# Output stores of a state-space convolution and gated-MLP kernel: one transfer over 128 partitions instead of four over 32

## The chip, the cores and the metric

One core of one Trainium2 chip. The metric is the device time of one execution in microseconds; of the kernel before there are three runs, and their median is used.

## The reference

The input `A_q` (here `x`) has 2,048 tokens of 640 numbers, in bfloat16. The result is the sum of three terms:

```python
x = A_q
xn = _layernorm(x, axis=-1)
return x + _A_ref(xn, A_k, A_v, A_shift_k, A_ssm_k, A_ssm_D) + _B_ref(xn, B_w_gate, B_w_up, B_w_down)
```

`_A_ref` shifts `k` over four tokens with weights, multiplies it by `v`, convolves each of the 640 channels over all 2,048 tokens by a Fourier transform, adds a skip term, and multiplies by `xn`. `_B_ref` is a gated MLP: `g = xn @ w_gate`, `u = xn @ w_up`, `h = sigmoid(g) * u`, `h @ w_down`, with 1,728 hidden columns. The output has the shape and type of `x`: 2,048 x 640 in bfloat16, 2.62 MB.

## The kernel before, in words

**Layout.** The tile `acc` (line 259) lives in SBUF during the whole kernel. It has 128 partitions, 16 token tiles `m` and 640 columns. It is loaded with `x`, the two branches are added into it, and at the end it is stored to the output. The tokens are not laid out in plain order: token = 64 n + 16 q + m, where n runs to 32, q to 4, m to 16, and the partition is p = 32 q + n. The convolution needs this order. One partition therefore holds 16 tokens that follow each other in DRAM, so that several token tiles of one partition form one run of bytes (1,280 bytes a tile). The views `xq4` and `oq4` of input and output are written so:

```python
xq4 = A_q.flatten_outer_dims().rearrange("(n q m) d -> q n m d", q=4, m=NQ)
oq4 = out.flatten_outer_dims().rearrange("(n q m) d -> q n m d", q=4, m=NQ)
```

In DRAM the row of partition (q, n) begins at 10240 q + 40960 n elements. Within one q all 32 rows have one distance; over all 128 partitions, two distances are needed.

**Stages.** TensorE runs two streams that are interleaved: the convolution as Fourier matrices (lines 508, 528, 580 and 612), and the MLP, four token groups of 512 tokens, each with 14 pieces of hidden columns (gate and up, line 770) and then the down projection (line 786). ScalarE and VectorE empty PSUM. What reaches `acc` last are VectorE's additions: line 621 adds the convolution's product for four token tiles and half the columns, and line 798 adds 320 columns of one token tile's down projection.

**Order.** Every operation is recorded with what it reads and writes, then emitted in the order of a list written out by hand (`ORDER`, lines 80 to 124), in which numbers 960 to 983 are the stores. So the order on each engine's queue is fixed. A DMA is issued by SyncE (queue SP), or by ScalarE (queue ACT) where `q="ACT"` is given. Each queue issues in order: an instruction that waits holds up all behind it. The framework hands out eight completion semaphores to the DMAs in turn, and a DMA waits until the transfer that had its semaphore before has completed.

**The stores.** `store` (line 626) is called six times (lines 891 to 896): token tiles 0 to 7, 8 to 11, 12 and 13, 14, and tile 15 in two halves of 320 columns. Each call issues four DMAs, one for each q, of 32 partitions; for the halves of tile 15, q = 1 and 3 are issued by ScalarE. In `ORDER` two of the four stores of tiles 8 to 11 stand late, among those of tile 14. On SyncE the built program has, in this order: one store of tiles 0 to 7, one of 8 to 11, three of 0 to 7, one of 8 to 11, four of 12 and 13, one of 14, one of 8 to 11, three of 14, one of 8 to 11, and four of tile 15. The first store of tile 14 has a completion semaphore that a ScalarE store of tile 15 uses before it.

**Two small loads with the same kind of view.** `load_D` (line 394) and `load_shift` (line 380) read views with the group g (4) outermost, into four partitions 32 apart:

```python
srow = A_shift_k.rearrange("(h g d) m -> g h (d m)", h=2, g=G)
drow = A_ssm_D.rearrange("(h g d) -> g h d", h=2, g=G)
```

**Other transfers that the text names.** `xnd<-xq` (line 692) writes the normalized tokens to a buffer in DRAM, from 128 partitions. `P<-S` (line 548) copies half a tile, 64 partitions, to the other half within SBUF. `w<-in_B_w_up_dram` and `w<-in_B_w_gate_dram` (line 378) load 512 columns of weights into 128 partitions, five runs each.

Of the kernel before, what the change touches and what calls it, by code (L numbers as in the profile page):

```python
# [15 lines left out]
ACT = mybir.ActivationFunctionType  # L16
# [26 lines left out]
def _dft_tables():  # L43
# [74 lines left out]
    395, 396, 545, 895, 921, 896, 907, 546, 900, 923, 908, 922, 910, 559, 924, 912, 547, 548, 560, 561, 563, 564, 562,  # L118
    565, 913, 566, 569, 567, 915, 909, 568, 570, 579, 911, 925, 580, 914, 933, 582, 917, 572, 916, 934, 581, 583, 935,
    919, 584, 573, 918, 575, 574, 576, 586, 920, 944, 577, 960, 938, 587, 939, 589, 945, 402, 593, 941, 588, 590, 591,  # L120
    966, 962, 594, 947, 936, 963, 596, 942, 937, 943, 595, 961, 597, 965, 598, 940, 946, 403, 970, 969, 948, 950, 949,
    952, 968, 951, 953, 954, 971, 956, 973, 967, 975, 974, 972, 955, 964, 957, 958, 979, 978, 976, 977, 959, 982, 983,
    981, 980
]
ON_DVE = [
    101, 103, 133, 134, 135, 136, 656, 658, 884, 875, 525, 518, 915, 570, 581, 575
# [93 lines left out]
def kernel(  # L220
# [17 lines left out]
    oq4 = out.flatten_outer_dims().rearrange("(n q m) d -> q n m d", q=4, m=NQ)  # L238
# [20 lines left out]
    acc = cst.tile([P, NQ, DM], BF16, name="acc")  # L259
# [61 lines left out]
    def dma(fn, nd, run, q="SP", **kw):  # L321
        few = 1.4 if nd <= 64 and run > 1000 else 1.0
        plan.op({q: (0.48 + nd / 8000.0, lambda: fn(nc.sync if q == "SP" else nc.scalar))},
                size=1.05 * few * nd * (10.6 + run / 23.8) / 16e3 + 0.03, **kw)
# [301 lines left out]
    def store(m0, m1, pri, d0=0, d1=DM):  # L626
        key = [("acc", m, x) for m in range(m0, m1) for x in range(4)] if d1 - d0 == DM else (
            [("fin", m, d0 // 320) for m in range(m0, m1)] + [("cv", m // 4) for m in range(m0, m1)])
        for q in range(4):
            dma(lambda e, q=q: e.dma_start(oq4[q][:, m0:m1, d0:d1], acc[32 * q:32 * q + 32, m0:m1, d0:d1]), 32,  # L630
                2 * (d1 - d0) * (m1 - m0), q="ACT" if m0 == 15 and q % 2 else "SP", r=key, w=[("out", m0, d0, q)], pri=pri)

    MEAN, VAR, RST, TMP, EPS = range(5)

# [247 lines left out]
    for tr in range(4):  # L882
# [5 lines left out]
        if tr < 3:  # L888
            rec_tp(tr + 1, gt())
        rec_down(tr, tr == 3)  # L890
    store(0, 8, 240.0)
    store(8, 12, 242.0)
    store(12, 14, 244.0)
    store(14, 15, 246.0)
    store(15, 16, 247.0, d1=320)
# [32 lines left out]
```

## Time and profile before

| | us |
|---|---|
| median of 3 runs | 259.51 (258.78 to 261.09) |
| profiled execution, its own time | 262.01 |
| its span, first to last instruction | 259.9 |
| TensorE busy | 244.0 (94%) |
| VectorE busy | 201.2 (77%) |
| ScalarE busy | 175.5 (68%) |
| last matmul ends, last addition ends | 252.2, 252.7 |
| mean granted TensorE clock | 0.978 |

The span is what the views of the profile count in: their times start with the first instruction. The profiled execution's own time is 2.1 us longer than its span. In its page one of 40 slices, before 182 us, has a granted TensorE clock of 0.5; the slices around it have 0.9 or more. Busy shares are over the whole span. A row of DMA issues gives the number of transfers of one size, the KB of each and the median time from issue to landing (the last completion); it gives none where no landing could be read. The share of 16 DMA engines is the time that packets took, divided by 16 times the stretch.

### The profile page before, as it was taken

The page shows a single profiled execution, that of the slowest core. Times are in us where ns is not written, and L with a number is a line of the kernel's source. Part 1 is how long each engine was busy: PE and PEld are TensorE (multiplying, and loading weights), DVE is VectorE, ACT ScalarE, POOL GpSimd, SP SyncE. Part 2 cuts the span into 40 slices and gives each one's busy share as a digit, 9 for nine tenths or more (in the row PEclk, how much of TensorE's full clock was granted, in tenths as well). Part 3 has the DMA queues.
Part 4 walks back from the last instruction along what each step waited for, and adds up shares of the span by engine and source line. Part 5 has one row for each costly group of instructions (what it writes and reads, how often), then busy time and mean ns, then how long its engine had stood idle before and what let it go on. Part 6 is the DMA issues. An engine that isn't in the chain of part 4 may idle for free.

```text
span 259.9 us, 9463 instructions
## 1 busy us (share of the span) xinstructions
PE 244.0 (94%) x4231; PEld 146.1 (56%) x4231; DVE 201.2 (77%) x337; ACT 175.5 (68%) x259; POOL 0.7 (0%) x6
## 2 busy tenths in 40 slices
PE   8999979999999999999999997899999999998980
PEld 2854436764445467666554554577676554556750
DVE  4623524768999899999999999579999998895630
ACT  3623779767888899788998885663899785441100
POOL 1000000000000000000000000000000000000000
PEclk9999999999999999999999999599999999999996
DMA  6999999999995528999999739934126476002823
GB/s 175 310 277 207 205 314 130 152 139 188 229 248 128 143 75 235 150 140 128 157 182 283 192 66 318 188 101 117 23 62 177 99 236 184 1 5 55 188 73 95
DMA packets 91024, 41.44 MB, mean 159 GB/s; under 512 B 66656, under 2 KB 88104, under 8 KB 90664
## 3 DMA queue, kind: packets, MB, share of 16 engines
q1 hardware_dynamic: 90600, 40.44, 73.6%
q8 instruction: 33, 0.54, 0.9%
q10 hardware_dynamic: 384, 0.41, 0.5%
q14 instruction: 7, 0.06, 0.1%
HBM read 30.61 MB, written 5.24 MB: 138 GB/s over the span
## 4 chain that ended last, share of the span: by engine, by line
PE 64%; DMA 18%; DVE 5%; SPq 4%; issue 3%; ACT 3%; DVEq 0%; ACTq 0%
PE g L786 25%; PE g L770 25%; DMA acc<-in_A_q_dram 9%; PE c L528 6%; DMA w<-in_B_w_up_dram 5%; DMA vt<-in_A_v_dram 3%; PE c L612 3%; PE c L580 3%; PE c L508 2%; DMA P<-S 2%; ACT S L314 1%; SPq L378 1%; SPq L352 1%; DVE hT L737 1%; SPq L827 1%
## 5 line engine op out<-in xcount | busy, mean ns | idle before, releaser
L770 PE MATMUL g<-xnT,w 128*128 128x512 bf16 x380 | 90.9, 379 | 2.6 <-ACT sig L735 1.3
L786 PE MATMUL g<-wd,hT 128*128 128x320 bf16 x448 | 68.5, 306 | 2.0 <-issue 2.0
L770 PEld LDWEIGHTS <-w 128*128 128x128 bf16 x380 | 34.7, 98 | 41.1 <-issue 2.6
L786 PEld LDWEIGHTS <-hT 128*128 128x128 bf16 x448 | 42.6, 99 | 19.4 <-issue 2.3
L314 ACT CAST S<-c 128x1024 bf16<-128x1024 f32 x40 | 39.4, 1026 | 8.1 <-PE c L528 8.0
L737 DVE TENSOR_TENSOR hT<-sig,g 128x512 bf16<-128x512 bf16 x32 | 21.9, 686 | 18.6 <-PE g L770 18.3
L770 PE MATMUL g<-xnT,V 128*128 128x512 bf16 x140 | 32.8, 379 | 0.0
L735 ACT ACTIVATE sig<-g 128x512 bf16<-128x512 f32 x32 | 19.2, 601 | 15.1 <-PE g L770 13.5
L798 DVE TENSOR_TENSOR acc<-g,acc 128x320 bf16<-128x320 f32 x32 | 15.5, 488 | 17.4 <-PE g L786 17.2
L528 PEld LDWEIGHTS <-Mt 64*128 64x128 f16 x1280 | 20.2, 96 | 8.7 <-issue 8.1
L528 PE MATMUL c<-T,Mt 64*128 64x64 bf16 x1280 | 22.8, 191 | 2.2 <-issue 2.2
L317 ACT ACTIVATE T<-c 128x1024 bf16<-128x1024 f32 x20 | 19.9, 1029 | 5.5 <-PE c L508 5.4
L770 PEld LDWEIGHTS <-V 128*128 128x128 bf16 x140 | 13.3, 98 | 15.7 <-DMA V<-in_B_w_up_dram 0.5
L488 DVE TENSOR_TENSOR kvt<-ta,vt 128x1024 bf16<-128x1024 bf16 x10 | 21.4, 2143 | 0.1
L314 ACT CAST V<-c 128x1024 bf16<-128x1024 f32 x18 | 18.2, 1026 | 3.2 <-PE c L580 3.1
L314 ACT CAST T<-c 128x1024 bf16<-128x1024 f32 x19 | 18.8, 1024 | 1.6 <-PE c L508 1.4
L729 ACT ACTIVATE sig<-g 128x512 bf16<-128x512 f32 x18 | 10.8, 602 | 5.0 <-PE g L770 3.3
L561 DVE TENSOR_TENSOR S<-S 128x1024 bf16<-128x1024 bf16 x20 | 13.8, 688 | 0.3
L475 DVE TENSOR_TENSOR ta<-ta,tb 128x1024 bf16<-128x1024 bf16 x20 | 13.8, 688 | 0.3
L470 DVE TENSOR_TENSOR tb<-kt,sT 128x1024 bf16<-128x1024 bf16 x20 | 13.8, 690 | 0.1
L567 DVE TENSOR_TENSOR S<-P 64x1024 bf16<-64x1024 bf16 x18 | 12.4, 689 | 0.6
L565 DVE TENSOR_TENSOR S<-S 64x1024 bf16<-64x1024 bf16 x18 | 12.4, 687 | 0.6
(82 smaller groups left out, 240.9 us busy)
## 6 DMA issues: line engine op xcount, KB each, us to landing
w<-in_B_w_gate_dram SPq DMA_DIRECT2D x7, 640.0 KB, 6.9
w<-in_B_w_up_dram SPq DMA_DIRECT2D x7, 640.0 KB, 5.2
P<-S SPq DMA_DIRECT2D x14, 256.0 KB, 3.7
kt<-in_A_k_dram SPq DMA_DIRECT2D x8, 320.0 KB, 6.3
vt<-in_A_v_dram SPq DMA_DIRECT2D x8, 320.0 KB, 7.1
xnd<-xq SPq DMA_DIRECT2D x4, 640.0 KB, 5.0
ht<-in_A_ssm_k_dram SPq DMA_DIRECT2D x16, 96.0 KB, 5.8
wd<-in_B_w_down_dram SPq DMA_DIRECT2D x3, 480.0 KB, 9.8
```

Of the source, the lines that this page charges most:

```text
L314: fa = lambda: nc.scalar.copy(out=out_fn(), in_=in_fn())
L317: fa = lambda: nc.scalar.activation(out_fn(), in_fn(), ACT.Copy, scale=scale)
L470: dve(1024, 2, lambda: nc.vector.tensor_tensor(tl[c][:], sl(tl[kb], 3 - m), sh(m), ALU.mult) if c != o else nc.vector.tensor_tensor(tl[c]. ...
L475: dve(1024, 2, lambda: nc.vector.tensor_tensor(tl[a][:], tl[a][:], tl[c][:] if c != o else tl[c].rearrange("p b n j -> p n b j"), ALU.add) ...
L488: dve(1024, 1 if kt else 2, lambda: nc.vector.tensor_tensor(by_j(tl[o]) if kt else tl[o][:], tl[a].rearrange(form), sl(tl[vb], 0).rearrang ...
L528: nc.tensor.matmul(tl[c][:, b, 64 * kk:64 * kk + 64], lhsT=Mb[rows, k, 64 - 64 * r:192 - 64 * r], rhs=tl[T][rows, 2 * k + r].rearrange("p ...
L561: dve(n, 2, lambda b=b: nc.vector.tensor_tensor(X(b), X(b), H(b), ALU.mult), r=[(Z, b, 0)] + sr, w=[(S_, "p", b)], pri=pri + 0.01)
L735: act(512, lambda: nc.scalar.activation(tl[sg][:], pv(0), ACT.Sigmoid), r=[pk(0)], w=[(sg,)], alloc=[(sg, "sig")], pri=pri - 2000)
L737: dve(512, 1, lambda: nc.vector.tensor_tensor(hT[:, fc, :], tl[sg][:], pv(1), ALU.mult), r=[pk(1), (sg,)], w=[(hk, fc)], pri=pri - 2000)
L770: nc.tensor.matmul(tl[c][:], lhsT=w()[:, k, o:o + P], rhs=tl[X][:, k, :], start=(k == 0), stop=(k == NC - 1))
L786: nc.tensor.matmul(tl[pd[i]][:, 0:320], lhsT=hT[:, fc, t4 * P:(t4 + 1) * P], rhs=wd[:, fc, 320 * i:320 * i + 320], start=(fc == 0), stop=( ...
L798: dve(320, 1, lambda i=i, m=m, pd=pd: nc.vector.tensor_tensor(acc[:, m, 320 * i:320 * i + 320], tl[pd[i]][:, 0:320], acc[:, m, 320 * i:320 ...
```

## The change

`store` issues one DMA over all 128 partitions where it issued four over 32, and SyncE issues all of them. Six stores remain (960 to 965 in `ORDER`). In the new order SyncE has: tiles 0 to 7, 12 and 13, 14, 8 to 11, and the two halves of tile 15. The built instruction of each has 128 partitions on the SBUF side and 4 x 32 rows on the DRAM side. The order of the instructions on the other engines stays as it was, but for the four DMAs that leave ScalarE's queue.

```diff
@@ ORDER, its last lines
-    966, 962, 594, 947, 936, 963, 596, 942, 937, 943, 595, 961, 597, 965, 598, 940, 946, 403, 970, 969, 948, 950, 949,
-    952, 968, 951, 953, 954, 971, 956, 973, 967, 975, 974, 972, 955, 964, 957, 958, 979, 978, 976, 977, 959, 982, 983,
-    981, 980
+    594, 947, 936, 596, 942, 937, 943, 595, 597, 598, 940, 946, 403, 948, 950, 949, 952, 962, 951, 953, 954, 956, 963,
+    955, 961, 957, 958, 964, 959, 965
@@ def store(m0, m1, pri, d0=0, d1=DM):
-        for q in range(4):
-            dma(lambda e, q=q: e.dma_start(oq4[q][:, m0:m1, d0:d1], acc[32 * q:32 * q + 32, m0:m1, d0:d1]), 32,
-                2 * (d1 - d0) * (m1 - m0), q="ACT" if m0 == 15 and q % 2 else "SP", r=key, w=[("out", m0, d0, q)], pri=pri)
+        dma(lambda e: e.dma_start(oq4[:, :, m0:m1, d0:d1], acc[:, m0:m1, d0:d1]), 128,
+            2 * (d1 - d0) * (m1 - m0), r=key, w=[("out", m0, d0, 0)], pri=pri)
```

## The prediction

> **What bounds the kernel now.** I read the views from the end backwards, because the change touches only the last stores. First the chain that ended last, from 250 us on (start, length, what):
>
> ```profile
> 249.99 2.19 PE g L786 x16
> 252.18 0.02 issue
> 252.21 0.49 DVE acc L798
> ```
>
> The chain of computation is TensorE's down projection up to 252.2 us and one VectorE addition to 252.7. The span is 259.9 us, so the last 7.2 us hold no computation at all. The timeline from 248 us shows what is there (start, length, engine, line, what, count; an issue row merges neighbours and so also covers their waits):
>
> ```profile
> 249.21 8.58 SPq L630 DMA_DIRECT2D out_dram<-acc  x12
> 251.25 0.49 DVE L798 TENSOR_TENSOR acc<-g,acc 128x320 bf16<-128x320 f32 x1 [2.36 <-PE g L786]
> ...
> 251.78 1.75 ACTq L630 DMA_DIRECT2D out_dram<-acc  x4
> 252.21 0.49 DVE L798 TENSOR_TENSOR acc<-g,acc 128x320 bf16<-128x320 f32 x1 [0.46 <-PE g L786]
> ```
>
> ```profile
> SPq L630 <- DMA out_dram<-acc: 5.3, 2, 3.2
> ```
>
> The second fence is SyncE's own waits after 245 us (total, times, longest). Twelve stores are issued by SyncE between 249.21 and 257.79. The longest wait, 3.2 us, ends at 253.2: the store of tile 14 shares its completion semaphore with an ACT store issued at 251.78 and waits until that has landed. Then ten issues follow at about 0.45 us each (253.29 to 257.79), the last lands at 258.88, and the closing semaphore waits and drains take 1.03 us more. So the tail is SyncE's serial issuing. That is what the edit shortens. What each store takes on the DMA engines is in the transfers from 234 us on (queue: packets, MB, share of 16 engines; then issues with KB each and us to landing):
>
> ```profile
> q1 hardware_dynamic: 960, 2.54, 41.3%
> q10 hardware_dynamic: 192, 0.08, 1.2%
> ...
> out_dram<-acc SPq DMA_DIRECT2D x4, 320.0 KB, 4.3
> out_dram<-acc SPq DMA_DIRECT2D x4, 160.0 KB, 2.2
> ```
>
> 20 SyncE stores make 960 packets and 4 ACT stores 192: 48 each, which the packet records split into 32 rows and 16 four-byte completion writes, one per DMA engine. Every store now runs on 16 engines.
>
> **The change part by part.** Removed: 14 of SyncE's 20 stores and all 4 of ACT's. The other engines' instructions keep their order, so computation still ends at 252.7 and costs nothing either way. Moved: the two halves of tile 15 come to SyncE alone, at the end, with nothing queued behind them; the store of tiles 8 to 11, ready at 240.68 when the addition of line 621 ends, now stands behind those of tiles 12 to 13 and 14, which wait for line 798 (248.89), so it is issued at about 249.5 instead of from 240.7. Only the end of the program waits for it. The shared-semaphore wait of 3.2 us goes: the six stores' semaphores were last used by transfers issued before 216 us. On issuing alone the six cost less: 0.37 us each by the 512-column weight loads that found the queue free, 0.60 us by the half-tile copies P<-S. I take 0.60; six are 3.6 us, and only the last one follows the last addition.
>
> What decides is how many DMA engines carry a store. A token tile's 128 partitions are p = 32q + n; in DRAM the row of (q, n) lies at 10240q + 40960n elements. Four separate stores each had 32 rows at one stride on both sides. The single store needs two strides in DRAM, so the built instruction carries 4 x 32 rows there and 128 partitions in SBUF. The only transfers of this trace whose outermost count is 4 are two small loads:
>
> ```profile
> Dt<-in_A_ssm_D_dram SPq DMA_DIRECT2D x1, 1.2 KB
> ...
> xq<-in_A_shift_k_dram SPq DMA_DIRECT2D x1, 5.0 KB
> ```
>
> They are shown without a time to landing, and the semaphore records say why: where other loads raise their semaphore 16 times as data lands, the D load gives one update just after its issue (14.99 us) and then four (19.43, 20.09, 20.54, 21.44); the shift load likewise one and four. They ran on four engines. They have 4 on both sides, the new store 4 and 128, so neither bound is excluded: 4 engines or 16. I take 4, the row with which it shares the outermost count in DRAM.
>
> [...]
>
> Next, the rate of one engine. Windows in which little but one kind of transfer moves (the last two columns are the share of 16 engines and GB/s):
>
> ```profile
> 98.60:100.40 1.80, 1.80 (x43) 1.24 (x41) 1.74 (x4) 1.80 (x3) 0.00 (x0) 1.00 1.05 350
> ...
> 180.00:181.40 1.40, 1.40 (x45) 0.90 (x43) 1.40 (x3) 0.29 (x1) 0.00 (x0) 1.00 0.98 202
> 244.00:246.00 2.00, 2.00 (x17) 1.46 (x15) 1.46 (x3) 0.00 (x0) 0.00 (x0) 1.00 1.10 241
> ```
>
> The first is the store xnd<-xq from 128 partitions: 350/1.05/16 = 20.8 GB/s an engine. The second is P<-S from 64 partitions: 202/0.98/16 = 12.9. The third is the present 32-partition stores: 241/1.10/16 = 13.7. A 10,240-byte packet mostly takes 0.78 us there and at best 0.385 (26.6 GB/s), so a full engine's rate is halved when 16 engines read only 32 or 64 partitions. With four engines, each gets one block of 32 partitions and they walk partitions n, 32+n, 64+n and 96+n in step. The nearest rows are the two halved ones: P<-S is halved although its 16 engines have 64 different partitions, so engines hinder each other across blocks of 32, and the third row is the same stores. I take their middle, 13.3 GB/s, and keep 12.9 and 26.6 as bounds.
>
> [...]
>
> The sum. The first store is released at 235.13 and issued at 235.15, as now; its first packet comes 0.85 us later (236.0). The output is 2.54 + 0.08 = 2.62 MB. Four engines move 4 x 13.3 = 53.2 GB/s: 49.3 us. The stream has no gap, since the first store alone (1.31 MB) keeps the four engines busy to 260.6, after all the others have been issued. Data ends at 285.3; completion 0.5 us (the store of 240.69: last packet 242.43, landed 242.93); closing 1.0. Span 286.8, 26.9 over the profiled 259.9. The profiled execution took 262.01, 2.1 beyond its span and 2.5 above the median of the runs; the difference goes on the median: 259.51 + 26.9 = **286.4 us**. The six issues and the 3.2 us wait, gains by themselves, vanish under it. Bounds: at 12.9 GB/s the stream takes 50.8 us, 287.9; at 26.6 it takes 24.6, 261.7.
>
> **Rivals.** *Sixteen engines, so faster.* For it: all other transfers of 128 partitions have 16. Against it: the four updates. Tile 14 is issued at 248.9, tiles 8 to 11 at 249.5; first packet 250.4, 0.66 MB at 333 GB/s (first window) to 206 (second) ends by 253.6. The last half tile is issued at 252.73, 0.6 us, and lands about 254.4, closing 255.4: 4.5 less, 255.0 us. The number of engines decides: the stream from 236.0 has to end by 258.4 to be no slower than now, 117 GB/s, nine engines at 13.3.
>
> *Four engines without halving.* If the four don't hinder each other, 20.8 GB/s each (the first window) gives 31.5 us, span 269.0, 268.6 us; its best is the 261.7 above. For it: four readers are few, and a lone straggler's packet did take 0.385. Against it: P<-S is halved with 64 partitions, so separate partitions don't keep engines apart.
>
> *Sixteen engines, but issued block by block.* If the generator takes each of the four blocks as an issue of its own, a store costs 4 x 0.6 = 2.4 us; from 248.9 four of them end at 258.5, landing and closing 2.5 later, 261.0: 260.6 us, no change that can be told. Against it: the weight loads have five blocks per partition and are issued in 0.37.
>
> **How the numbers follow.** Forecast 0.70, halved four engines. Unhalved 0.15. Sixteen engines 0.11. Block by block 0.04. About 1% (2.6 us) is what a measurement of this kernel can tell from no change. Slower: 0.70 plus 0.13 of the unhalved case; within 1%: 0.04 and 0.02; faster 0.11. The range runs from the unhalved bound, 262, to the slow bound 287.9 plus the spread of the runs above their median (1.6), 290; it leaves out sixteen engines, blocks and a little of the rest, under 2 in 10. The forecast's own range is 283 to 290.
>
> **What would show it.** Right: from 234 us on, 132 packets a store (128 rows and 4 completions), about 53 GB/s at a share of 0.25, TensorE still ending near 252 and some 34 us of stores alone. The count of four engines is wrong if there are 144 packets a store and the end lies near 255; the rate is wrong if the share is 0.25 with more than 80 GB/s. The issue rows should be below 0.7 us unless the queue is full.

## The result, and the profile after

The change makes the kernel slower: 270.19 us (median of 4 runs, 269.48 to 271.60) against 260.28 us (258.78 to 261.09) for the kernel before on the same chip, a ratio of 1.039 with a 95% interval of 1.032 to 1.047. That is 9.9 us more. Here and below each ratio is to the kernel before on the same chip; ratios and their intervals are of fast runs alone (a run more than 1.5% above the fastest of its kernel is left out), medians are of all runs. The forecast was 286.4 us, 26.9 more: slower, as forecast, but by little more than a third of the amount.

The timeline of the changed kernel from 247 us (start, length, engine, line, what, count; an issue row merges neighbours):

```profile
246.18 9.95 SPq L628 DMA_DIRECT2D out_dram<-acc  x3
...
248.88 0.49 DVE L796 TENSOR_TENSOR acc<-g,acc 128x320 bf16<-128x320 f32 x1 [0.46 <-PE g L784]
```

The last addition ends at 249.37, but the span ends at 268.66. The 19.3 us between them hold no computation; before it was 7.2. SyncE's waits show what fills it (total, times, longest):

```profile
SPq L628 <- DVE acc L620: 28.6, 2, 18.5
SPq L921 <- DMA out_dram<-acc: 11.5, 1, 11.5
```

The 11.5 us are the closing wait for the last store to land. The waits for another store's semaphore, 5.3 us before, are gone, as forecast. The packets that the six stores made, from 230 us on:

```profile
q1 hardware_dynamic: 792, 2.62, 17.8%
```

792 is six times 132: 128 rows and 4 completions a store. So the stores run on four DMA engines. Stretches of the stream, whose first packet comes at 233.20 (the last two columns are the share of 16 engines and GB/s):

```profile
235.00:237.00 2.00, 2.00 (x121) 1.49 (x120) 1.71 (x3) 0.53 (x1) 0.00 (x0) 1.00 0.20 51
237.00:241.00 4.00, 4.00 (x68) 2.93 (x55) 2.80 (x5) 1.29 (x2) 0.00 (x0) 1.00 0.27 81
241.00:245.00 4.00, 4.00 (x31) 2.88 (x30) 1.81 (x3) 0.00 (x0) 0.00 (x0) 1.00 0.26 101
245.00:249.00 4.00, 3.85 (x29) 2.54 (x26) 1.10 (x3) 0.00 (x0) 0.00 (x0) 1.00 0.28 74
249.00:253.00 4.00, 0.00 (x0) 0.00 (x0) 0.37 (x1) 0.00 (x0) 0.00 (x0) 1.00 0.23 65
...
257.00:261.00 4.00, 0.00 (x0) 0.00 (x0) 0.00 (x0) 0.00 (x0) 0.00 (x0) 0.50 0.25 104
```

Four busy engines of 16 are a share of 0.25, and from 237 to 261 it is 0.23 to 0.28. In the first stretch shown they move 51 GB/s, about what the forecast had for the whole stream. But from 241 on the same four engines move 101. (The dip to 74 and 65 that follows is taken up under "One store earlier".) The stream runs from 233.20 to 267.13, 33.9 us instead of 49.3: 2.62 MB / 33.9 us / 4 = 19.3 GB/s an engine where 13.3 was taken. Why the rate does not stay low is what the experiments had to settle.

The start of the stores differs by some microseconds between executions (230.97 to 235.15 us in these profiles). So executions are compared below from the issue of the first store to the end of the span: 24.8 us before, 36.7 after.

### The profile page after: what moved, and what is told of

Read it like the earlier page. It is cut to its first block, busy times and chain, and to the rows that moved or that the text cites. A ratio compares the mean times of both kernels' runs of the same rounds, so it can differ in the third digit from the quotient of the medians.

```text
span 268.7 us, 9442 instructions
## 1 busy us (share of the span) xinstructions
PE 241.7 (90%) x4231; PEld 145.2 (54%) x4231; DVE 201.3 (75%) x337; ACT 175.3 (65%) x259; POOL 0.7 (0%) x6
## 4 chain that ended last, share of the span: by engine, by line
PE 80%; DMA 4%; ACT 4%; issue 2%; DVE 1%; ACTq 0%; DVEq 0%
PE g L768 38%; PE g L784 24%; PE c L527 7%; PE c L611 4%; DMA w<-in_B_w_up_dram 3%; PE c L579 3%; PE c L507 2%; ACT S L313 1%; DMA acc<-in_A_q_dram 1%; PE c L748 1%; PE g L703 1%; ACT T L316 1%; ACTq L351 0%; ACT V L313 0%; ACT sig L727 0%
## 5 line engine op out<-in xcount | busy, mean ns | idle before, releaser
L784 PE MATMUL g<-wd,hT 128*128 128x320 bf16 x448 | 67.0, 302 | 1.2 <-issue 1.2
L768 PEld LDWEIGHTS <-w 128*128 128x128 bf16 x380 | 34.8, 98 | 39.8 <-DMA w<-in_B_w_up_dram 2.2
L733 ACT ACTIVATE sig<-g 128x512 bf16<-128x512 f32 x32 | 19.2, 599 | 15.1 <-PE g L768 13.5
L313 ACT CAST V<-c 128x1024 bf16<-128x1024 f32 x18 | 18.2, 1025 | 3.2 <-PE c L579 3.1
L727 ACT ACTIVATE sig<-g 128x512 bf16<-128x512 f32 x18 | 10.8, 600 | 5.0 <-PE g L768 4.0
L560 DVE TENSOR_TENSOR S<-S 128x1024 bf16<-128x1024 bf16 x20 | 13.7, 687 | 0.3
L474 DVE TENSOR_TENSOR ta<-ta,tb 128x1024 bf16<-128x1024 bf16 x20 | 13.7, 687 | 0.3
L469 DVE TENSOR_TENSOR tb<-kt,sT 128x1024 bf16<-128x1024 bf16 x20 | 13.8, 688 | 0.1
```

The source lines that it names most:

```text
L313: fa = lambda: nc.scalar.copy(out=out_fn(), in_=in_fn())
L469: dve(1024, 2, lambda: nc.vector.tensor_tensor(tl[c][:], sl(tl[kb], 3 - m), sh(m), ALU.mult) if c != o else nc.vector.tensor_tensor(tl[c]. ...
L474: dve(1024, 2, lambda: nc.vector.tensor_tensor(tl[a][:], tl[a][:], tl[c][:] if c != o else tl[c].rearrange("p b n j -> p n b j"), ALU.add) ...
L560: dve(n, 2, lambda b=b: nc.vector.tensor_tensor(X(b), X(b), H(b), ALU.mult), r=[(Z, b, 0)] + sr, w=[(S_, "p", b)], pri=pri + 0.01)
L733: act(512, lambda: nc.scalar.activation(tl[sg][:], pv(0), ACT.Sigmoid), r=[pk(0)], w=[(sg,)], alloc=[(sg, "sig")], pri=pri - 2000)
L768: nc.tensor.matmul(tl[c][:], lhsT=w()[:, k, o:o + P], rhs=tl[X][:, k, :], start=(k == 0), stop=(k == NC - 1))
```

## The experiments

**The number of engines, in the whole kernel.** One number in the view of the output is changed, so that each store is still one transfer over 128 partitions, with another outermost count in DRAM:

```diff
-oq4 = out.flatten_outer_dims().rearrange("(n q m) d -> q n m d", q=4, m=NQ)
+oq4 = out.flatten_outer_dims().rearrange("(n q m) d -> q n m d", q=16, m=NQ)
```

and likewise 8 and 2.

> The changed kernel with the output viewed with q = 16 instead of 4: each store is still one transfer over 128 partitions with two strides in DRAM, issued by SyncE in the same order, but the outer count in DRAM is 16. The rows land in permuted places of the output, which is the only part that changes. Theory N (the outer count in DRAM sets the number of DMA engines, and that number sets the tail): 144 packets a store (128 rows and 16 completions), the last landing about 1.7 us after the last addition, time 255 to 257 us, about 4 us under the kernel before. Rival F (the form of the store, two strides in DRAM against 128 partitions, is slow by itself or slow to issue): 268 to 271 us as for the change.

> The same with q = 8 (rows permuted again). Theory N: 136 packets a store, eight engines; at the 19.3 GB/s an engine that the changed kernel shows (2.62 MB in 33.9 us on four) the stream takes 17 us from the first store, so it ends with the computation and the tail is set by the last half tile: 255 to 258 us. Rival F: 268 to 271 us.

> The same with q = 2 (rows permuted). Theory N: 130 packets a store, two engines, a stream of 49 us (at 26.6 GB/s an engine) to 68 us (at 19.3): 285 to 304 us. Rival F: 268 to 271 us.

The packets of the version with 16, after 225 us:

```profile
q1 hardware_dynamic: 864, 2.62, 15.4%
```

That is 6 x 144; with 8 there are 816, 6 x 136, and with 2 there are 780, 6 x 130: sixteen, eight and two completions a store. These three versions write the rows to other places of the output; they time the transfer and can't replace the kernel. In these four versions the outermost count in DRAM sets the number of engines, and the number of engines orders the times:

| outermost count | median us | ratio to before | first issue to end, us |
|---|---|---|---|
| 16 | 254.65 | 0.982 (0.973 to 0.991) | 20.5 |
| 8 | 258.92 | 0.996 (0.990 to 1.001) | 28.2 (in an execution of 261.91) |
| 4 (the change) | 270.19 | 1.039 (1.032 to 1.047) | 36.7 |
| 2 | 288.45 (one run) | 1.11 (no interval) | 55.0 |

With sixteen engines the rival "sixteen engines, so faster" of the prediction comes true nearly to the number (255.0). So the transfer over 128 partitions and the single queue do no harm by themselves (254.65 us against 260.28 before). With eight the time was at the upper end of what was expected (255 to 258) or a little above it.

**The stores alone.** No computation; the stores of eight token tiles into scratch, each started when the one before has landed. The changed kernel's form is `outer("d_o4", 4)`:

```python
def outer(name, q, p0=0, p1=P, m1=8):
    turn()    # a small VectorE operation that waits for the store before
    v = view(name, q * P // (p1 - p0)) if p1 - p0 == P else view(name, P // ((p1 - p0) // q))
    nc.sync.dma_start(v[0:q, :, 0:m1, :], acc[p0:p1, 0:m1, :])
```

> Leaves out all computation: it loads x in plain order, stores eight token tiles (rows of 10,240 bytes) in twelve ways one after the other, each waiting for the one before, and writes x as output. In order: 128 partitions plain; four times 32 partitions; outer count 16, 8, 4, 2; outer count 4 with the DRAM rows of a block side by side; partitions 0 to 63 with outer count 2; partitions 32 to 95 with outer count 2; partitions 0 to 31 with outer count 4; outer count 4 with rows of 2,560 bytes; outer count 4 again. [...] Rival D (rows that lie 20 to 80 KB apart in DRAM hinder each other): 0.77 us for outer 4, 0.385 for side by side rows, and no difference between partitions 0 to 63 and 32 to 95. Rival C (the computation beside it slows the stores): 0.385 us everywhere with four engines or fewer.

In its timeline each VectorE row names the store that it waited for, in brackets, with the wait; it is one to two microseconds longer than the data took. In order: a plain transfer over the 128 partitions, with one distance in DRAM; sixteen engines, eight, four, two; four engines with the rows side by side in DRAM; two engines on partitions 0 to 63, and on 32 to 95:

```profile
14.97 0.17 DVE L36 TENSOR_SCALAR acc<-acc 128x2 bf16<-128x2 bf16 x1 [4.58 <-DMA d_plain<-acc]
...
30.34 0.17 DVE L36 TENSOR_SCALAR acc<-acc 128x2 bf16<-128x2 bf16 x1 [7.70 <-DMA d_o<-acc]
42.26 0.17 DVE L36 TENSOR_SCALAR acc<-acc 128x2 bf16<-128x2 bf16 x1 [11.75 <-DMA d_o<-acc]
60.68 0.17 DVE L36 TENSOR_SCALAR acc<-acc 128x2 bf16<-128x2 bf16 x1 [18.24 <-DMA d_o<-acc]
87.23 0.17 DVE L36 TENSOR_SCALAR acc<-acc 128x2 bf16<-128x2 bf16 x1 [26.38 <-DMA d_o<-acc]
105.64 0.17 DVE L36 TENSOR_SCALAR acc<-acc 128x2 bf16<-128x2 bf16 x1 [18.24 <-DMA d_near<-acc]
124.03 0.17 DVE L36 TENSOR_SCALAR acc<-acc 128x2 bf16<-128x2 bf16 x1 [18.22 <-DMA d_lo<-acc]
138.48 0.17 DVE L36 TENSOR_SCALAR acc<-acc 128x2 bf16<-128x2 bf16 x1 [14.28 <-DMA d_mid<-acc]
```

By the packets the data took 5.97, 10.04, 16.62 and 24.79 us for 16, 8, 4 and 2 engines: 13.7, 16.3, 19.7 and 26.4 GB/s an engine. The four stores over 32 partitions of the kernel before took 5.97 us together, as long as the one with sixteen. The plain transfer, which has 16 completions too, took 3.28 us, 25.0 GB/s an engine: sixteen engines need not hinder each other, so more counts than their number; the tests below point to which partitions they read at the same time. Four engines on partitions 0 to 31, by division 8 each, took 3.55 us (23.1 GB/s an engine); four on all partitions with rows of 2,560 bytes took 5.85 us (14.0). Three things follow. A rate like the kernel's 19.3 is there without any computation (19.7), so computation does not set it. It is the same with rows side by side in DRAM, so the distance in DRAM does not set it. And two engines on partitions 0 to 63 reach 19.7 each, on 32 to 95 26.1, with a DRAM side of the same form: between these two stores it is the partitions read in SBUF that make the difference, so engines do hinder each other there. So the rivals C and D of the expectation fall. The forecast's half rate for a whole stream falls as well: 13.3 GB/s is 0.77 us for every row of 10,240 bytes, where with eight and four engines the median row took 0.45 and 0.385. So the hindrance does not last all the time. The store with four engines shows this over its length (windows of this run, last columns as above):

```profile
43.80:47.00 3.20, 0.00 (x0) 0.00 (x0) 1.00 0.23 51
47.00:50.00 3.00, 0.00 (x0) 0.00 (x0) 1.00 0.23 68
...
53.00:56.00 3.00, 0.00 (x0) 0.00 (x0) 1.00 0.24 99
```

The packet records don't name the engine; packets that follow each other without a gap are taken as one engine's. Such a series of rows of 10,240 bytes takes 0.75, 0.78, 0.78, 0.97, then 0.39, 0.39, 0.52, 0.95, then 0.39, 0.39, 0.39, 0.73, and 0.39 from there on. Another, which lags, takes 0.72 to 0.79 for its first seven rows and about 0.4 from the fourteenth on. The durations change in groups of four rows. The two leading engines end 1.4 to 1.8 us, about four rows, before the two others.

**How long the halving lasts.** Again stores alone, of a larger tile, with rows of 10,240 bytes unless said:

```python
turn(); outer("d_twoa"); outer("d_twob")          # four engines, two stores back to back
turn(); outer("d_wide", 15)                       # four engines, rows of 19,200 bytes
turn(); rows("d_r1", 16, 1)                       # 16 engines, 8 rows an engine
turn(); rows("d_r2", 16, 2); turn(); rows("d_r6", 16, 6)   # 16 and 48 rows an engine
```

> No computation of the reference: stores into scratch, one after the other, source one tile in SBUF, the output is a copy of A_q. Theory (engines whose blocks lie 32 partitions apart halve each other only while they walk in step, about the first 12 rows of 10,240 bytes at 0.76 us, after which a row takes 0.385): one store with four engines 16.6 us; two of them back to back 28.9 if they stay out of step from one store to the next, 33.2 if each starts anew; the same with rows of 19,200 bytes (32 rows an engine) 27.6 if the time decides, 31.6 if the number of rows does; sixteen engines with 8, 16 and 48 rows each: 6.0, 10.7 and 23.0 us (220, 245 and 342 GB/s). Rival (the number of engines sets the rate, 13.7 GB/s an engine with sixteen and 19.7 with four, however long they run): 16.6, 33.2, 31.2, and for sixteen engines 6.0, 12.0 and 35.8 us, all three 220 GB/s.

The waits of the two stores back to back, of the wide one, and of the three with sixteen engines:

```profile
72.67 0.17 DVE L41 TENSOR_SCALAR big<-big 128x2 bf16<-128x2 bf16 x1 [30.44 <-DMA d_twob<-big]
109.77 0.17 DVE L41 TENSOR_SCALAR big<-big 128x2 bf16<-128x2 bf16 x1 [36.93 <-DMA d_wide<-big]
117.59 0.17 DVE L41 TENSOR_SCALAR big<-big 128x2 bf16<-128x2 bf16 x1 [7.65 <-DMA d_r<-big]
131.78 0.17 DVE L41 TENSOR_SCALAR big<-big 128x2 bf16<-128x2 bf16 x1 [14.02 <-DMA d_r<-big]
171.74 0.17 DVE L41 TENSOR_SCALAR big<-big 128x2 bf16<-128x2 bf16 x1 [39.78 <-DMA d_r<-big]
```

The single store of this run ran beside loads that were still going and says nothing. The data of the two back to back took 28.8 us, as the theory had it (28.9) and not 33.2: engines that are out of step stay so from one store to the next. But with sixteen engines the data took 5.96, 12.35 and 38.1 us. There the theory fell (6.0, 10.7, 23.0) and the rival was nearly right (6.0, 12.0, 35.8): after 48 rows the halving was still there (12.9 GB/s an engine). The wide rows, 35.3 us, missed all three numbers. So a number of rows is not what ends the halving.

A narrower theory, the author's estimate from these rows, fits most of them. The durations change in groups of four rows, so two engines on blocks 32 partitions apart would halve each other only while both are in the same group of four of their blocks. It leaves out the two pairs that were hardly slowed: blocks 64 partitions apart (outermost count 2, 26.4 GB/s an engine) and partitions 32 to 95 (26.1). With four engines each has 32 rows, eight groups. A leading series gains 0.3 to 0.4 us on a lagging one in each of the second, third and fourth group (2.24 against 2.62 us, 1.90 against 2.30, 1.56 against 1.87); after that nearly every row of both takes about 0.4. With sixteen engines each has 8 partitions, by division, two groups, so there is one border to get ahead at. With wide rows the lead of one group is a longer time. The last two points were only argued, and the 35.3 us were not worked out from them; the first can be tested. One thing the theory leaves open: in the second group of the store on partitions 0 to 63 the leader's first two rows take 0.385 us while the other's take 0.72 and 0.75, so the two do not halve each other row by row.

**Blocks of another length.** If that is so, the halving must vanish from the first row on when the blocks are 36 partitions long rather than 32, since the partner then is one group ahead. Stores alone, two engines (at the end four), rows of 10,240 bytes:

```python
def blocks(name, q, n):
    turn()
    v = dr.tile([q, n + 1, 8 * DM], BF16, name=name)
    nc.sync.dma_start(v[:, 0:n, :].rearrange("q n (m d) -> q n m d", m=8), acc[0:q * n, 0:8, :])
```

> No computation of the reference: stores into scratch one after the other, rows of 10,240 bytes (a row takes 0.385 us alone, 0.76 halved); the output is a copy of A_q. Each store has two (or four) engines, each walking one block of 28 to 40 neighbouring partitions, so at the same moment the engines read partitions that lie as far apart as the block is long. Theory (two engines halve each other only while both read the same group of four partitions modulo 32 and of the same half, which is why the times in the traces change in groups of four rows): blocks of 28: 28 x 0.385 = 10.8 us; of 32: 16.6 as measured; of 33: between 13 and 17; of 34: between 13.1 and 17; of 36 and of 40, one or two groups ahead from the first row: 13.9 and 15.4; four engines with blocks of 28: 10.8, with blocks of 32: 16.6. Rival (engines reading the same half of the partitions hinder each other at their start whatever the row, some 4.3 us for twelve rows): 15.1, 16.6, 17.0, 17.4, 18.2, 19.7, and 15.1 and 16.6 with four.

The waits for two engines with blocks of 28, 32, 34 and 36 partitions, and for four with 28 and 32:

```profile
22.98 0.17 DVE L36 TENSOR_SCALAR acc<-acc 128x2 bf16<-128x2 bf16 x1 [12.83 <-DMA d_2x<-acc]
41.37 0.17 DVE L36 TENSOR_SCALAR acc<-acc 128x2 bf16<-128x2 bf16 x1 [18.23 <-DMA d_2x<-acc]
...
76.14 0.17 DVE L36 TENSOR_SCALAR acc<-acc 128x2 bf16<-128x2 bf16 x1 [16.85 <-DMA d_2x<-acc]
92.36 0.17 DVE L36 TENSOR_SCALAR acc<-acc 128x2 bf16<-128x2 bf16 x1 [16.05 <-DMA d_2x<-acc]
...
122.94 0.17 DVE L36 TENSOR_SCALAR acc<-acc 128x2 bf16<-128x2 bf16 x1 [12.91 <-DMA d_4x<-acc]
141.35 0.17 DVE L36 TENSOR_SCALAR acc<-acc 128x2 bf16<-128x2 bf16 x1 [18.24 <-DMA d_4x<-acc]
```

| blocks | data, us | theory | rival |
|---|---|---|---|
| 2 x 28 | 11.05 | 10.8 | 15.1 |
| 2 x 32 | 16.62 | 16.6 | 16.6 |
| 2 x 33 | 15.89 | 13 to 17 | 17.0 |
| 2 x 34 | 15.17 | 13.1 to 17 | 17.4 |
| 2 x 36 | 14.39 | 13.9 | 18.2 |
| 2 x 40 | 15.67 | 15.4 | 19.7 |
| 4 x 28 | 11.20 | 10.8 | 15.1 |
| 4 x 32 | 16.62 | 16.6 | 16.6 |

More rows take less time, from 32 rows to 36, and four engines with blocks of 28 move 102 GB/s where four with blocks of 32 move 79. The rival falls. What the runs show is this: with blocks of 28 and 36 partitions, so that by division the engines read rows 28 and 36 partitions apart, the data took 11.05 and 14.39 us, close to 0.385 us a row (10.8 and 13.9), and with blocks of 32 it took 16.62, 4.3 us above that (12.3). What the theory says of 32 and of halves rests on these times and on two of the stores above (0 to 63 at 19.7 GB/s an engine, 32 to 95 at 26.1). Why a distance of 32 partitions costs this time, no run shows.

**All on SyncE, in the new order, but with four stores over 32 partitions.** Against the kernel before, the stores stand in the changed kernel's order, and:

```diff
-                2 * (d1 - d0) * (m1 - m0), q="ACT" if m0 == 15 and q % 2 else "SP", r=key, w=[("out", m0, d0, q)], pri=pri)
+                2 * (d1 - d0) * (m1 - m0), q="SP", r=key, w=[("out", m0, d0, q)], pri=pri)
```

> One part of the change alone: the stores stay four over 32 partitions, as before, but all 24 are issued by SyncE and stand in the order of the changed kernel (tiles 8 to 11 behind those of 12 to 13 and 14). Theory (the number of engines decides, queue and order cost nothing): 240 waits go, SyncE issues four of tile 14 from 248.9, four of tiles 8 to 11, four and four half tiles, 16 at 0.45 us = 7.2, to 256.1; landing 1.6 and closing 1.0 later the span is 258.7, median about 258.3, ratio 0.99 to 1.00, same. Rival (a good part of the 9.9 us comes from leaving ScalarE's queue and the early place of tiles 8 to 11): 262 us or more, ratio above 1.01.

257.14 us, ratio 0.996 (0.992 to 1.001). Its timeline:

```profile
247.01 5.00 SPq L630 DMA_DIRECT2D out_dram<-acc  x10
247.61 0.49 DVE L798 TENSOR_TENSOR acc<-g,acc 128x320 bf16<-128x320 f32 x1 [0.46 <-PE g L786]
```

From the first issue to the end it took 23.2 us, 1.6 less than before. Ten issues follow each other without a wait for a semaphore of another store. So with stores on sixteen engines the queue and the order cost nothing that the runs resolve, and the loss of the change belongs to the form of the transfer.

**One store earlier.** The changed kernel, with the store of tiles 8 to 11 issued right after its data is ready:

```diff
-    ... 952, 962, 951, 953, 954, 956, 963, 955, 961, 957, 958, 964, 959, 965
+    ... 952, 961, 962, 951, 953, 954, 956, 963, 955, 957, 958, 964, 959, 965
```

> The changed kernel with one thing moved: the store of tiles 8 to 11 stands ahead of those of tiles 12 to 13 and 14, so it is issued right after 240.7 and not near 249. Theory (four engines have one gapless stream, so the order inside it does not count): 270 us as in the changed kernel, within 1 us, ratio to the kernel before 1.035 to 1.045. Rival (the stream waits for late stores): 2 us or more less, 268 or below.

It took 268.01 us (ratio 1.037, 1.031 to 1.043), on the edge between the two expectations, so it was run again beside the changed kernel itself:

> The changed kernel itself, beside the next one. Theory: 270.2 as before, from the release of the first store to the end 36.7 us.

> The changed kernel with the store of tiles 8 to 11 ahead of those of tiles 12 to 13 and 14, on the same chip as the changed kernel itself. Its first look took 268.0 us and 34.8 from the first release to the end, against 270.2 and 36.75; the stretch of 1.7 us in the last row of the first store, seen in the changed kernel, was gone. If the order costs about 2 us by that row, it comes out 2 us below the changed kernel again and the row shows in one and not in the other; if the order counts for nothing, both are within 1 us.

The changed kernel took 270.13 us (1.041, 1.035 to 1.047) and the other 269.65 (1.037, 1.032 to 1.042). The difference of 0.5 us is not resolved. In the profiled executions, first issue to end, it is 36.1 against 34.8 us, and the packet records put it near the end of the first store: in the changed kernel, both times, six rows take 1.7 to 2.6 us, each engine's last row among them, while in the other version the last rows take 0.5 to 0.9. This is the dip to 74 and 65 GB/s of the changed kernel. What stretches these rows was not found. Whether it is the order that does it, 1 to 2 us at most, stays open.

**A version to beat both.** Since the tail before was serial issuing, the cure is fewer groups, not wider transfers: four stores over 32 partitions in three groups.

```diff
-    store(0, 8, 240.0)
-    store(8, 12, 242.0)
-    store(12, 14, 244.0)
-    store(14, 15, 246.0)
-    store(15, 16, 247.0, d1=320)
-    store(15, 16, 248.0, d0=320)
+    store(0, 12, 242.0)
+    store(12, 15, 246.0)
+    store(15, 16, 248.0)
```

> A version meant to beat both: four stores over 32 partitions as before (16 engines each), but three groups instead of six (tiles 0 to 11, 12 to 14, 15), so 12 stores, and SyncE and ScalarE share those of tiles 12 to 14 and of 15. Theory (the tail of the kernel before is serial issuing): last addition 252.7, two issues on each queue to 253.6, the last lands 1.6 after its issue starts, 254.8, closing 1.0: span 255.9, 4.0 less, median about 255.5, ratio 0.985. If the transfers themselves were the limit (1.97 MB from 240.7 at 241 GB/s would end at 248.9, 0.49 MB more by 251, 0.16 MB more by 254.5) it would be no earlier than 256. Rival (the first group starting at 240.7 and not 235.1 makes the stream late): 259 or more.

As it ran, ScalarE issued only two stores of tile 15 (the line with `m0 == 15 and q % 2` was as before), and SyncE all of tiles 12 to 14. It took 255.61 us (255.5 was expected), ratio 0.987 (0.982 to 0.992). The tail of its timeline:

```profile
251.26 0.49 DVE L797 TENSOR_TENSOR acc<-g,acc 128x320 bf16<-128x320 f32 x1 [0.46 <-PE g L785]
251.78 2.00 SPq L629 DMA_DIRECT2D out_dram<-acc  x2
251.78 0.85 ACTq L629 DMA_DIRECT2D out_dram<-acc  x2
```

SyncE's two issues take 2.00 us where ScalarE's two take 0.85: SyncE's second waits until 253.45 for ScalarE's first, with which it shares a semaphore. The next version takes that away:

```diff
-q="ACT" if m0 == 15 and q % 2 else "SP"
+q="ACT" if m0 >= 12 and q % 2 else "SP"
```

> The version with three groups of four 32-partition stores again, but now SyncE and ScalarE do share the stores of tiles 12 to 14 as well as those of tile 15 (in the one before, SyncE issued all of tiles 12 to 14). That changes which stores share a completion semaphore: the last SyncE store waited for ScalarE's first of tile 15 (until 253.45, 1.2 us after SyncE was free at 252.2), and now shares with a store of the first group that has long landed. Theory: the last issue ends 0.85 us after the last addition, lands 1.5 after it started, closing 0.9: the end 3.0 us after the last addition where it was 4.15: 1.1 less than that version, median about 254.5, ratio 0.982. Rival (the transfers are the limit): no less than 255.6.

```profile
252.69 0.49 DVE L797 TENSOR_TENSOR acc<-g,acc 128x320 bf16<-128x320 f32 x1 [0.46 <-PE g L785]
253.20 0.78 SPq L629 DMA_DIRECT2D out_dram<-acc  x2
253.21 0.85 ACTq L629 DMA_DIRECT2D out_dram<-acc  x2
```

The last store no longer waits. SyncE's first store of tile 15 waits 2.3 us for ScalarE's first of tiles 12 to 14, but that ends at 253.0, just before its data is ready (253.18), so it costs next to nothing. From the last addition to the end it is 3.3 us instead of 4.2 (7.2 before). In the time the version cannot be told from the one before it: 256.26 us, ratio 0.988 (0.983 to 0.993). The 254.5 of the theory was missed, and the rival (no less than 255.6) stands; that the transfers are the limit there was not tested further. Both versions are faster than the kernel before, by some 3 us, and faster than the change by 14.

## Why the prediction was right or wrong

**The number of engines was right.** Four, read from the semaphore updates of two small loads. The 132 packets a store and the share of 0.25 are as forecast, and the runs with 16, 8 and 2 show that the outermost count, and with it this number, makes the change slower: with 16 the same single transfers on SyncE are no slower than the kernel before.

**The step that failed is the rate of one engine.** The term was 13.3 GB/s; it measured 19.3, so the stream took 33.9 us and not 49.3, which is 15.4 of the 16.2 us between forecast and result. The prediction said that the four engines walk partitions n, 32+n, 64+n and 96+n "in step" and took the halved rate for the whole stream. The hindrance was right, and its size too: 51 GB/s from 235 to 237 us against 53 forecast. But the engines do not stay in step. After three to four groups of four rows the long rows end, and in the store alone nearly every row takes 0.385 us from then on. The rows that the rate was taken from could not show this. P<-S reads 64 partitions with sixteen engines and the old stores 32 with sixteen, so an engine has four partitions or two (by division; the records don't name them) and, by the estimate above, never leaves its group; of the stores alone, one with sixteen engines stayed halved for 48 rows (12.9 GB/s an engine). A rate of 12.9 to 13.7 was carried from transfers in which, by that estimate, an engine cannot get ahead to one in which the rows show that it does.

**What the 33.9 us are made of**, by the packet records, a mean over the four engines: 655 KB an engine at the best rate of 26.6 GB/s are 24.6 us; the halved rows at the start add 3.4 (15.7 us for the 32 rows of the store alone against 12.3); the same rows take 2.6 more in the kernel (18.3), nearly all of it the six stretched rows, whose cause is open; the smaller rows of the later stores add 1.5 (13.8 against 12.3). That is 32.1, and the engines do not all start and end together.

**The rival "four engines without halving"** gave 268.6 us and is nearest in time. Its mechanism is not what happened: the engines did halve each other, and its 20.8 GB/s came from a transfer with sixteen engines. It came close because the average over halved and free rows, 19.3, happens to lie there.

**The small terms.** The first packet came 1.27 us after the issue instead of 0.85, completion took 0.46 (0.5 forecast), closing 1.07 (1.0). The order of the stores costs nothing that the runs resolve, as said. The shared-semaphore wait vanished, and, as said, its 3.2 us did not show in the time. The issue rows were forecast below 0.7 us "unless the queue is full", and they did grow while the four engines were behind (that the queue was full is not shown by itself): the first of tile 15's two issues took 5.8 us, from 248.45 to 254.23, and the wait for its data, at most to 249.37, explains 0.9 of them. It delayed nothing that shows, since the four engines had work all the time.

**The test that the prediction named** gave the right answer: a share of 0.25 with more than 80 GB/s was to mean that the rate is wrong, and from 241 to 245 the window shows 101 at 0.26.

## What to carry to other kernels

Before several transfers are merged into one, look at the outermost count on the DRAM side: a transfer over 128 partitions whose DRAM side begins with a dimension of 4 ran on four of the 16 engines here (a share of 0.23 to 0.28), and the time from the last addition to the end grew from 7.2 to 19.3 us. A rate that is read from a trace is that of the transfers in it: 13.3 GB/s an engine was read here, and 19.3 measured in the new transfer. Before a rate is carried over, ask whether the engines can get out of each other's way in the new transfer. When the tail is serial issuing, fewer groups on two queues shorten it without touching the number of engines: 7.2 us became 4.2 and 3.3 here, and the time fell by some 3 us.

## What the runs showed of the hardware that was not expected

- Engines that start in step on blocks 32 partitions apart get out of step by themselves: the long rows of 10,240 bytes (0.65 to 0.97 us) lie almost all in the first 13, and from there nearly every row takes 0.385, also in the next store on the same queue (two stores of 1.31 MB in 28.8 us, one alone in 16.6). Why the leader gains was not tried.
- Blocks of 28, 36 or 40 partitions nearly avoid the halving: two engines took 11.05, 14.39 and 15.67 us for them, where 0.385 us a row makes 10.8, 13.9 and 15.4; with blocks of 32 they took 16.62.
- With sixteen engines on blocks of 8 partitions the halving lasts: 12.9 GB/s an engine over 48 rows each (7.86 MB in 38.1 us). It is not sixteen engines as such: the plain transfer over 128 partitions moved 1.31 MB in 3.28 us where the one with outermost count 16 took 5.97.
- An issue on a queue whose four engines were behind took at least 4.9 us beyond any wait for data, where it took 0.64 on a free one (the first store, 231.93 to 232.57).
